# Another order for a two-layer decode kernel: other pairs, other slots, 29 filler matmuls fewer

## The chip, the cores and the metric

The kernel runs on one core of one Trainium2 chip. The metric is the device time of one execution in microseconds (us). TensorE multiplies, VectorE, ScalarE and GpSimd (POOL in the profile) work on vectors, and SyncE (SP) issues the transfers from HBM. Each engine runs its own list of instructions in order and waits on semaphores.

## The reference

Four tokens go through two layers that share their weights. A layer is attention over the last 2048 positions of a key and value cache, and then a gated feed-forward network (FFN). Cut to what matters:

```python
B, D, Hq, Hkv, Dh, W, F = 4, 448, 16, 8, 256, 2048, 1792     # bfloat16
def A(x):                                  # attention, one new position per token
    q = (x @ wq).reshape(B, Hq, Dh)
    k, v = k_cache[:, :, -W:], v_cache[:, :, -W:]            # 8 heads, each for two q heads
    p = softmax(q . k * Dh ** -0.5)
    return (p . v).reshape(B, Hq * Dh) @ wo
def F(x):
    return (silu(x @ w_gate) * (x @ w_up)) @ w_down
for layer in range(2):
    x = x + A(layernorm(x))
    x = x + F(layernorm(x))
```

Both layers read the same caches. For one token and one key-value head the keys are 1 MB and the values 1 MB, so all four tokens and eight heads are 64 MB, more than the on-chip memory holds. A part of what layer 0 has loaded is kept for layer 1, the rest is loaded a second time.

## The kernel before

**Names.** A head's work is written with three digits, token, layer, head: 305 is token 3, layer 0, head 5; 315 is the same head in layer 1. Its keys are K305 and its values the halves V305.0 and V305.1, 512 KB each. Keys come as one load of 1 MB (K305) or as two halves (K305.0, K305.1).

**Groups and steps.** The list PLAN gives the steps; a step has one or more groups, and a group is one head or a pair. In a pair joined by `+` both heads' scores are one run of 32 matmuls; in a pair joined by `&` each member's scores are an instruction block of its own (16 matmuls each), so that the first can start, and give back its keys' slots, before the second's keys are there. For each group:

- VectorE transposes each half of the keys in place (L887, 32 by 32 blocks).
- TensorE makes the scores (L920); VectorE, TensorE and VectorE find and spread the maximum (L936, L941/L944, L950); ScalarE takes the exponential (L954); TensorE turns the probabilities (L969), ScalarE copies them (L978), TensorE and VectorE sum them (L986, L992).
- TensorE multiplies by the values, 8 matmuls for each half (L1001): "the first and second value product".
- ScalarE and VectorE copy the result out (L1017, L1019), TensorE flips it (L1025), VectorE scales it (L1035), and TensorE projects it by the output weights, in columns (L1047) or rows (L1055).

When a token's last head of a layer is projected, its row is added up (L794, L796, L804, L808, L812), normed (L555 to L581; on TensorE L561, "nstat", and L569, "nxe"), and goes through the FFN, as a row (L678 to L706; tokens 1 and 2) or in columns (L740 to L776), and after layer 0 through the next norm and query projection (L615, L621, L631, L638, L647). Token 2 and 3's layer 1 needs that projection's result.

**Slots.** Keys and values live in 31 slots of 512 KB; 7 more are the query weights' place and come free after the last query projection. SLOTS gives, for each load in turn, the slot (a whole key takes two adjacent ones). A load waits until the last reader of the slot's old content is done: the scores for keys, a value product for values. HOLD lists what layer 0 keeps for layer 1 (k keys, v a value half).

**Orders.** SEQ_PE, SEQ_DVE, SEQ_ACT, SEQ_POOL and SEQ_SP list, for each engine, every operation by its number, worked out beforehand and written out. A `w` with a number in SEQ_PE is a filler: one matmul with zero weights and 512 columns into the accumulator A, which adds nothing (L1137, and L543 where a filler follows a filler). The number says between which two uses of A by other engines it has to stand. SyncE issues the loads strictly in order, so a load whose slot isn't free holds up all loads behind it. The wait for a slot is made here:

```python
        for o in order[SP]:
            if o.cells:
                s0 = int(next(slots))
                for s, cell in enumerate(o.cells, s0):
                    cell.append(s)
                    if held[s] is not None:
                        o.deps[last[id(held[s])]] = True
                    elif s >= NPOOL:
                        o.deps.update((d, True) for d in late)
                    held[s] = cell
                self._count(o, f"h{s0}")
```

A whole key is issued at L875, a half at L881, a value half at L897.

Of the kernel before, what the change touches and what calls it, by code (L numbers as in the profile page):

```python
# [43 lines left out]
)  # L44
HOLD = (
# [3 lines left out]
)  # L49
WHOLE = (  # L50
    "000 001 002 003 004 005 006 007 010 011 012 014 100 101 102 103 104 106 107 110 114 116 117 202 203 204 205 "
    "206 207 211 213 215 216 301 302 304 306 307 311 312 313"
# [1149 lines left out]
```

## Time and profile before

| | |
|---|---|
| time, median of 3 runs | 278.19 us (277.27 to 281.54) |
| profiled execution | 280.76 us |
| its span, first to last instruction | 279.0 us |
| mean granted TensorE clock | 0.977 |
| read from HBM | 101.81 MB, 365 GB/s over the span |
| busy: TensorE, VectorE, ScalarE, GpSimd | 244.6, 184.9, 63.5, 80.0 us |
| of TensorE: fillers, 142 and 180 | 54.4 and 53.4 us |
| of VectorE: 86 transpositions of key halves | 104.9 us |

The page gives the whole span in 40 slices: the share that each engine is busy in tenths, the clock that TensorE was granted, and what the transfers moved. A busy TensorE says little, since fillers count as busy. The rows of a stretch give, for each engine, busy us and the number of instructions, then the granted clock, the busy share of the transfer engines and GB/s. The chain of work that ended last gives start, duration and what it was. A group's row gives line, engine, operation, tiles, shape and count, then busy us and the mean ns of one.

### The profile page before, as it was taken

The numbers are of one execution on the slowest core, as the hardware profiler recorded it, in microseconds if no ns is written. First come the engines' busy times: TensorE is split into PE (matmuls) and PEld (weight loads), VectorE is DVE, ScalarE is ACT, GpSimd is POOL, SyncE is SP. The second block draws the span as 40 slices with busy tenths as digits, with TensorE's granted clock in tenths as the row PEclk, the third lists the DMA queues.
The fourth block names the chain that finished last, engine by engine and source line by source line (L and its number), as shares of the span: only waits on it lengthen the run. The fifth ranks groups of instructions, "written<-read, shape, count | busy, mean of one in ns | idle before, by whom it ended". The sixth has DMA issues, their size and how long they took to land.

```text
span 279.0 us, 10606 instructions
## 1 busy us (share of the span) xinstructions
PE 244.6 (88%) x4767; PEld 125.9 (45%) x4587; DVE 184.9 (66%) x574; ACT 63.5 (23%) x173; POOL 80.0 (29%) x223
## 2 busy tenths in 40 slices
PE   3998999889999897999899798898969888998895
PEld 0121232223475454545454344454635547566664
DVE  4666817825702687888948489679678956588941
ACT  0003020101112222332233133123322322232411
POOL 1071021111114222515132432142322334143440
PEclk9999999999999999999999799799998999999998
DMA  7999999999999999999999999999999997899300
GB/s 279 429 416 413 412 398 422 397 400 409 398 392 415 411 411 415 411 406 414 365 414 385 422 414 412 406 325 399 361 375 421 405 391 270 320 403 417 138 2 3
DMA packets 25884, 102.49 MB, mean 367 GB/s; under 512 B 2539, under 2 KB 6639, under 8 KB 21487
## 3 DMA queue, kind: packets, MB, share of 16 engines
q1 hardware_dynamic: 25831, 101.83, 92.4%
q8 instruction: 36, 0.59, 0.9%
q14 instruction: 9, 0.07, 0.1%
q10 hardware_dynamic: 8, 0.00, 0.0%
HBM read 101.81 MB, written 0.00 MB: 365 GB/s over the span
## 4 chain that ended last, share of the span: by engine, by line
PE 23%; DVE 13%; DMA 9%; issue 3%; ACT 2%; POOL 1%; SPq 0%; ACTq 0%
DVE half L887 7%; DMA half<-in_A_v_cache_dram 6%; PE S L920 5%; PE Y L1001 5%; PE A L1137 3%; DMA half<-in_A_k_cache_dram 3%; DVE oh L1019 2%; PE A L543 2%; PE Y L969 1%; PE A L1047 1%; PE Z L740 1%; PE A L1055 1%; ACT wide L621 1%; DVE wide L796 1%; PE Z L615 1%
## 5 line engine op out<-in xcount | busy, mean ns | idle before, releaser
L887 DVE STREAM_TRANSPOSE half<-half 128x1024 uint32<-128x1024 uint32 x86 | 104.9, 1230 | 9.9 <-DMA half<-in_A_k_cache_dram 9.8
L1137 PE MATMUL A<-identb,small 128*128 128x512 bf16 x142 | 54.4, 393 | 3.9 <-DVE A L447 2.9
L1015 POOL TENSOR_TENSOR small<-small 128x2 f32<-128x2 f32 (+1 forms) x48 | 38.4, 803 | 60.9 <-DVE small L992 42.3
L543 PE MATMUL A<-identb,small 128*128 128x512 bf16 x180 | 53.4, 395 | 0.0
L920 PE MATMUL S<-half,qe 128*8 128x128 bf16 (+1 forms) x1536 | 43.8, 243 | 5.7 <-DVE half L887 3.0
L1001 PE MATMUL Y<-half,pT 128*8 128x256 bf16 (+1 forms) x1024 | 43.1, 275 | 4.1 <-DMA half<-in_A_v_cache_dram 1.6
L920 PEld LDWEIGHTS S<-half,qe 128*8 128x8 bf16 x1536 | 29.9, 85 | 20.3 <-DVE half L887 10.7
L954 ACT ACTIVATE praw<-S,small 104x128 bf16<-104x128 f32 (+1 forms) x48 | 19.3, 402 | 79.0 <-DVE small L950 74.9
L1019 DVE SCALAR_TENSOR_TENSOR oh<-oh,small,Y 128x256 bf16<-128x256 bf16 x48 | 22.5, 469 | 15.7 <-ACT oh L1017 15.5
L926 POOL TENSOR_TENSOR qe<-qc,tiny 128x64 bf16<-128x64 bf16 x64 | 18.1, 292 | 47.8 <-PE S L920 35.5
L1017 ACT ACTIVATE oh<-Y 128x256 bf16<-128x256 f32 x48 | 18.4, 382 | 47.0 <-PE Y L1001 36.8
L1001 PEld LDWEIGHTS Y<-half,pT 128*8 128x8 bf16 (+1 forms) x1024 | 19.3, 84 | 17.8 <-issue 5.6
L1137 PEld LDWEIGHTS A<-identb,small 128*128 128x128 bf16 x142 | 14.7, 103 | 17.8 <-issue 10.9
L978 ACT ACTIVATE pT<-Y 128x64 bf16<-128x64 f32 (+1 forms) x48 | 12.4, 257 | 35.0 <-PE Y L969 28.5
L1055 PE MATMUL A<-wo_sb,oT 128*4 128x448 bf16 x188 | 16.5, 360 | 1.8 <-DMA wo_sb<-in_A_wo_dram 1.3
L577 POOL TENSOR_SCALAR st<-st 128x1 f32<-128x1 f32 x16 | 4.2, 265 | 47.6 <-DVE st L567 43.3
L992 DVE TENSOR_REDUCE small<-Y 128x2 f32<-128x32 f32 (+1 forms) x48 | 9.0, 190 | 9.6 <-PE Y L986 8.5
L1082 POOL MEMSET oT<- 128x16 bf16 x38 | 4.1, 111 | 32.3 <-PE A L1055 26.7
L950 DVE TENSOR_REDUCE small<-S 104x1 f32<-104x32 f32 x48 | 8.4, 176 | 6.2 <-PE S L944 6.1
L1035 DVE TENSOR_TENSOR oT<-Y,small 128x4 bf16<-128x4 f32 (+1 forms) x63 | 9.0, 154 | 5.0 <-PE Y L1025 2.1
L936 DVE TENSOR_REDUCE tiny<-S 104x1 bf16<-104x128 f32 (+1 forms) x24 | 7.7, 323 | 5.2 <-PE S L920 5.0
L986 PEld LDWEIGHTS Y<-pT,tiny 128*128 128x128 bf16 x64 | 5.3, 98 | 12.4 <-ACT pT L978 5.9
(139 smaller groups left out, 272.6 us busy)
## 6 DMA issues: line engine op xcount, KB each, us to landing
half<-in_A_v_cache_dram SPq DMA_DIRECT2D x85, 512.0 KB, 11.1
half<-in_A_k_cache_dram SPq DMA_DIRECT2D x31, 1024.0 KB, 11.5
half<-in_A_k_cache_dram SPq DMA_DIRECT2D x24, 512.0 KB, 9.6
wo_sb<-in_A_wo_dram SPq DMA_DIRECT2D x8, 448.0 KB, 17.1
half<-in_A_wq_dram SPq DMA_DIRECT2D x3, 1024.0 KB, 8.7
wd_sb<-in_B_w_down_dram SPq DMA_DIRECT2D x1, 1568.0 KB, 18.4
wg_sb<-in_B_w_gate_dram SPq DMA_DIRECT2D x1, 1344.0 KB, 18.0
wu_sb<-in_B_w_up_dram SPq DMA_DIRECT2D x1, 1344.0 KB, 21.0
```

What stands on the lines that cost most here:

```text
L543: return e.add_instruction(mybir.InstMatmult(start_tensor_calc=start, stop_tensor_calc=stop, ldweights=load, name=nc.get_next_instruction_ ...
L887: return e.transpose(a, a)
L920: last = e.matmul(Sb[s_][qd:qd + 8, 0:32 * 2 * J], lhsT=qe[q_][:, P, ce, :, :].rearrange("p a n -> p (a n)"), rhs=keys(kcs[P], J * x, J, c ...
L926: g.op(POOL, "qe", lambda e, P=P, t=t, kvh=kvh: e.tensor_tensor(qe[q_][:, P, :, :, :], qc[t][:, kvh, :, :].unsqueeze(2).broadcast_to([128, ...
L954: return e.activation(praw[0:R, 0:N].rearrange("p (g r l) -> p g r l", g=J, l=2), Sb[s_][0:R, 0:N].rearrange("p (l g r) -> p g r l", l=2, ...
L978: g.op(SCA, f"pt{n}", lambda e: e.activation(pf, Yb[p_][:, 0:PW], ACT.Copy), r=(f"yp{p_}",), w=(f"pT{pt}",), bank=(f"Y{p_}",))
L1001: last = e.matmul(Yb[p_][32 * gg:32 * gg + M, 256:512], lhsT=pT[pt][:, gg, 2 * a + hv, 4 * P:4 * P + M] if n == 2 else pf[:, 16 * gg + 8 * ...
L1015: g.op(POOL, f"pow{n}", lambda e: e.tensor_tensor(ri[p_][:, 0:2 * n], rs[p_][:, 0:2 * n], expo[:, 1:1 + 2 * n], op=ALU.pow), r=(f"rs{p_}", ...
L1017: g.op(SCA, "oh", lambda e: e.activation(oh[:, :], Yb[p_][:, 256:512], ACT.Copy), r=(f"y{p_}",), w=("oh",), bank=(f"Y{p_}",))
L1019: g.op(DVE, "oho", lambda e: e.scalar_tensor_tensor(out=oh[:, :], in0=oh[:, :], scalar=lomask[:, 0:1], in1=Yb[p_][:, 256:512], op0=ALU.mul ...
L1055: last = e.matmul(Ab[32 * k:32 * k + B, 0:D], lhsT=oT[oi][:, k % 2, k // 2, :], rhs=wo_sb[:, 4 * kvh + k, :], start=False, stop=False, ski ...
L1137: return e.matmul(Ab[:, 0:512], lhsT=w, rhs=rhs, start=False, stop=False, skip_group_check=True)
```

## The change

Only the lists change. In PLAN, two pairs become `&` pairs (117 with 204, 215 with 217) and four become `+` pairs (213 with 216, 214 with 301, 212 with 111, 210 with 310); 203 and 115, and 110 and 305, are now steps of their own. In HOLD, v351 goes and v021 comes: V315.1 is loaded again and V012.1 isn't. In WHOLE, the loads of K110, K206 and K312 become halves, and those of K305, K300, K303, K210, K310 and K315 become whole; the other names that come and go there are of held keys, which aren't loaded. 85 value halves are loaded before and after; whole keys go from 31 to 34, half keys from 24 to 18. The fillers go from 322 to 293. The orders and slots are the same up to the slot of the 38th load; the order of the loads is the same up to the 81st.

```diff
 PLAN = (
     "005+001", "002+000", "006", "007", "003+004", "101 102", "100", "017+015", "016&014", "107 013", "103 105",
-    "106", "104", "010", "202", "201", "200 012", "113&114", "117+204", "203 115", "116", "205", "206 207",
-    "011 302", "110 305", "300", "213&216", "214&301", "303", "215+217", "304", "306+307", "112 211 212&111",
-    "313+317", "314+316", "210&310", "311", "315+312",
+    "106", "104", "010", "202", "201", "200 012", "113&114", "117&204", "203", "115", "116", "205", "206 207",
+    "011 302", "110", "305", "300", "213+216", "214+301", "303", "215&217", "304", "306+307", "112 211 212+111",
+    "313+317", "314+316", "210+310", "311", "315+312",
 )
 HOLD = (
-    "k03 ... v351 v360 v361 v370 v371"
+    "k03 ... v001 v021 v030 ... v360 v361 v370 v371"
 )
 WHOLE = (
-    "... 110 114 116 117 202 203 204 205 206 207 211 213 215 216 301 302 304 306 307 311 312 313"
+    "... 013 014 ... 107 114 117 202 203 204 205 207 210 211 214 217 300 301 302 303 304 305 306 307 310 315 316 317"
 )
 SLOTS = (
-    "0 2 5 13 18 26 7 15 20 28 4 3 10 12 25 23 8 5 17 16 13 14 2 26 7 15 20 26 27 20 4 5 6 21 29 30 26 20 4 6 0 1 "
+    "0 2 5 13 18 26 7 15 20 28 4 3 10 12 25 23 8 5 17 16 13 14 2 26 15 4 20 5 6 26 27 20 22 29 21 6 26 20 0 5 22 "
...
 )
```

SEQ_PE, SEQ_DVE, SEQ_ACT, SEQ_POOL and SEQ_SP are new from the place on where the two programs part, in the second half and a little before. Read back into names, the loads from the 82nd on are, before:

```
V012.1 V012.0 K204 K203 V204.0 V204.1 K205 V205.0 V203.0 V203.1 K206 V205.1 K207 K011 K302 V206.0 V206.1 V207.1
V207.0 K110 V011.0 K305.0 K305.1 V011.1 V302.0 K300.1 K300.0 V302.1 V110.0 V110.1 V305.0 K301 V305.1 V300.1 V300.0
K304 K303.0 V303.0 K303.1 K306 V301.1 V301.0 V303.1 K307 K112.1 K112.0 V306.1 V304.1 V304.0 V307.0 V306.0 V307.1
V211.0 V112.0 K212.0 K111.1 V112.1 K212.1 K111.0 K210.0 V211.1 V212.0 K210.1 V111.0 V212.1 V111.1 K310.0 K315.1
V310.0 K310.1 K315.0 V315.0 K312 V210.0 V210.1 V312.0 V312.1
```

and after:

```
V012.0 K204 V203.1 K203 V203.0 V207.0 K205 K206.1 V204.1 V204.0 V205.0 V205.1 K206.0 V206.0 K207 K011 K302 V206.1
V207.1 K110.1 V011.0 V011.1 K110.0 K305 K300 V302.0 V302.1 V110.0 V110.1 V305.0 K301 V305.1 V303.0 V300.1 K303 V300.0
K304 K306 V301.1 V301.0 V303.1 V306.0 K307 V307.1 V304.0 K112.0 V304.1 V306.1 K112.1 V307.0 K111.0 K212.1 K212.0 V211.0
V112.0 K111.1 V112.1 K210 V212.0 V211.1 V212.1 V111.0 V111.1 K310 K315 K312.0 V210.1 K312.1 V210.0 V310.0 V312.0 V315.0
V312.1 V315.1
```

What frees the slots of the loads that the prediction speaks of (S the scores, P the value products of a group):

| load | before | after |
|---|---|---|
| V200.1 | P of 202 | P of 202, second half |
| K204 | S of 012 | S of 200 and P of 201, first half |
| V203.1 | P of 200 | P of 201, second half |
| K301 | P of 302 and S of 305 | S of 305 |
| K303 | halves: P of 110, P of 300 | S of 300 |
| K304 | S of 300 | P of 305, both halves |
| V304.0 | S of 215+217 | P of 213+216, first half |
| K111.0 | S of 211 | S of 217 |
| K210 | halves: S of 112, S of 212 | P of 112, first half, and S of 112 |
| V211.1 | S of 211 | S of 211 |
| V315.1 | not loaded | P of 211, first half |

On TensorE, after token 3's last layer-0 value products, the order before is: scores of 112, column projections, scores of 211, nstat, first value product of 112, the FFN with nxe in it, second value product of 112. After it is: scores of 112 ahead of the last of token 3's value products, column projections, scores of 211, nstat, nxe, first value product of 112, the FFN's first part, second value product of 112. On VectorE, before, one half of K210 is transposed before and one after the row addition of token 1 (L796) that follows the last query projection; after, both are transposed before it.

More of the change, by code (lines that the diff above doesn't have):

```diff
@@ L40 @@
     "005+001", "002+000", "006", "007", "003+004", "101 102", "100", "017+015", "016&014", "107 013", "103 105",
[3 rows of a table removed]
[3 rows of a table added]
 )
 HOLD = (
[3 rows of a table removed]
[3 rows of a table added]
 )
 WHOLE = (
-    "000 001 002 003 004 005 006 007 010 011 012 014 100 101 102 103 104 106 107 110 114 116 117 202 203 204 205 "
-    "206 207 211 213 215 216 301 302 304 306 307 311 312 313"
+    "000 001 002 003 004 005 006 007 010 011 012 013 014 100 101 102 103 104 106 107 114 117 202 203 204 205 207 "
+    "210 211 214 217 300 301 302 303 304 305 306 307 310 315 316 317"
 )
```

115 rows, old and new, of tables (HOLD, SEQ_ACT, SEQ_DVE, SEQ_PE) are left out of this document.

## The prediction

> **What bounds the kernel now.** I read the page first, then the stream of loads by stretches, then the chain of work that ended last.
>
> ```profile
> span 279.0 us, 10606 instructions
> PE 244.6 (88%) x4767; PEld 125.9 (45%) x4587; DVE 184.9 (66%) x574; ACT 63.5 (23%) x173; POOL 80.0 (29%) x223
> PEclk9999999999999999999999799799998999999998
> DMA  7999999999999999999999999999999997899300
> GB/s 279 429 416 413 412 398 422 397 400 409 398 392 415 411 411 415 411 406 414 365 414 385 422 414 412 406 325 399 361 375 421 405 391 270 320 403 417 138 2 3
> q1 hardware_dynamic: 25831, 101.83, 92.4%
> half<-in_A_v_cache_dram SPq DMA_DIRECT2D x85, 512.0 KB, 11.1
> half<-in_A_k_cache_dram SPq DMA_DIRECT2D x31, 1024.0 KB, 11.5
> half<-in_A_k_cache_dram SPq DMA_DIRECT2D x24, 512.0 KB, 9.6
> ```
>
> The kernel reads 101.83 MB through one queue at about 412 GB/s, so a load of 512 KB (a unit from here on) takes 524288 B / 412 GB/s = 1.27 us. Each slice of the GB/s row is 279.0 / 40 = 6.98 us. The bytes run out in slice 37 (138 of about 412 GB/s, so after a third of it, 258.1 + 2.3 = 260.4 us); the last 18 us are computation. The stream is not full everywhere. Taken by stretches, with an undisturbed one first:
>
> ```profile
> 100.00:120.00 20.00, 17.26 (x412) 9.76 (x404) 16.72 (x44) 5.66 (x19) 6.54 (x17) 1.00 1.02 412
> 132.50:153.50 21.00, 19.00 (x388) 10.04 (x382) 15.51 (x45) 6.27 (x16) 5.11 (x16) 1.00 0.99 389
> 181.00:188.00 7.00, 6.65 (x152) 3.50 (x146) 5.49 (x19) 1.88 (x5) 3.52 (x11) 1.00 0.94 321
> 195.00:209.00 14.00, 11.09 (x253) 6.99 (x248) 9.30 (x27) 4.17 (x10) 4.47 (x14) 0.97 1.00 369
> 230.00:244.00 14.00, 12.92 (x336) 9.33 (x333) 8.28 (x34) 2.88 (x8) 4.19 (x13) 1.00 0.84 293
> ```
>
> The last number is GB/s. Against 412 the four stretches lose 21 × 23/412 = 1.2 us, 7 × 91/412 = 1.5, 14 × 43/412 = 1.5 and 14 × 119/412 = 4.0: 8.2 us in all. A hole appears where a load can't be issued because its slot is freed late, and the chain shows the same from the other side:
>
> ```profile
> 198.48 7.96 DMA half<-in_A_k_cache_dram
> 212.10 9.52 DMA half<-in_A_v_cache_dram
> 230.37 0.59 PE S L920 x29
> 231.83 7.86 DMA half<-in_A_v_cache_dram
> 239.73 0.42 PE Y L1001 x8
> ```
>
> The pieces at 198.48, 212.10 and 231.83 are K303.1, V304.0 and V211.1. The scores of 211 end at 230.96, SyncE then issues K111.0, K210.0 and V211.1, and TensorE goes on with 211 at 239.73. So the second half is bound by a loop: computation frees a slot, SyncE issues, the load lands 8 us later, computation goes on.
>
> **How late a load may be issued.** Two stretches in which the queue had run nearly dry give the time from issue to landing (last column):
>
> ```profile
> half<-in_A_v_cache_dram SPq DMA_DIRECT2D x4, 512.0 KB, 5.5
> half<-in_A_v_cache_dram SPq DMA_DIRECT2D x1, 512.0 KB, 7.3
> ```
>
> They are the four values issued at 181 to 184 us and V303.0, issued at 197.90. So the slot of a load must be free 5.5 to 7.3 us ahead of its turn. With 1.27 us a unit I can read the new order of loads for risk: count the units between the newest load that the freeing instruction, or one before it on its engine, needs, and the landing of the load that reuses the slot. Seven units are 8.9 us and leave 1.6 to 3.4 us for the computation between; four are 5.1 us and leave less than nothing. From V201.0 on, the old order has 19 loads with seven units or fewer, the new one 17.
>
> **The change part by part.**
>
> (a) *The exchanged half.* V002.1 now stays until 012 uses it, so V012.1 is not loaded, and V315.1 is loaded as the very last unit. The bytes are the same. All loads between come one unit, 1.27 us, sooner: **−1.3 us** for everything that waits on them. The price is one slot fewer up to about 144 us. V315.1 at the end is hidden if its landing stays ahead of the products of 315+312, which the chain has at 265.58 (row below), 5 us after the last bytes now. Without that cover it costs up to its 1.27 us. If the sooner stream waits for computation instead, the part gives 0.
>
> (b) *The holes at 181 to 209*, 3.0 us. K303.1 waited for the values of 300, and V304.0 for the scores of 215+217. K303 as a whole load now waits only for the scores of 300, and V304.0 takes a slot of the values of 213+216, a few microseconds sooner. But V110.0, V305.1, V303.0, V300.1 and K304 still stand seven units behind what frees them; K304 is moved behind both values of 305. All 3.0 may go, or these five may lose 1.5 more than now; I take a third of the hole, **−1.0 us**.
>
> (c) *The hole at 230 to 244*, 4.0 us. The old queue stood behind the scores of 112 and of 211. In the new one K210 (1 MB) waits for the first value product of 112, four units behind V112.0 and nine behind V307.0, token 3's last layer-0 value. Its delay from these rows (V306.0 is the value landing at 224.2; 112's two products are the last rows):
>
> ```profile
> 224.20 0.83 PE L1001 MATMUL Y<-half,pT 128*8 128x256 bf16 x24
> 231.54 0.39 PE L1001 MATMUL Y<-half,pT 128*4 128x256 bf16 x8
> 233.02 0.39 PE L1001 MATMUL Y<-half,pT 128*4 128x256 bf16 x8
> ```
>
> Now it ends 231.93 − 224.20 = 7.7 us after token 3's last values begin. The new order has fewer fillers before it but puts the second norm matmul (nxe) ahead of it; working the same steps with their present durations I get 6.7. K210 can then land at 6.7 + 5.5 to 7.3 + 1.27 (its second unit) = 13.5 to 15.3 us; its turn is at 9 × 1.27 = 11.4. The hole is 2.1 to 3.9 us; I take 3.3, **−0.7 us**. Bounds: −4.0 if the product ends within 3 us, and +3 if it ends at 10. Everything behind K210 moves with it.
>
> (d) *The tail.* From 248 us the chain goes through VectorE's transpositions of the last keys:
>
> ```profile
> 248.31 0.61 DVE L796 TENSOR_TENSOR wide<-A,wide 128x448 bf16<-128x448 f32 x1
> 249.35 1.23 DVE L887 STREAM_TRANSPOSE half<-half 128x1024 uint32<-128x1024 uint32 x1
> 260.37 1.23 DVE L887 STREAM_TRANSPOSE half<-half 128x1024 uint32<-128x1024 uint32 x1
> 265.58 1.05 PE Y L1001 x32
> 276.35 0.28 DVE wo_sb L819
> ```
>
> Between 248.31 and 261.60 VectorE does seven transpositions with hardly a gap. In the new order both of K210 stand ahead of the row of 248.31, so six are left: **−1.2 us**, if K210 lands in time for that, else 0. The keys of 312 come two units sooner, which VectorE hides; a hole in (c) grown by 3 us would uncover them. From 265.58 on nothing changes: 13.4 us to the end.
>
> (e) *29 fillers fewer.* 26 of them stood between the first token's FFN row and the next query projection of token 2, 137 to 202 us: 46 before, 20 after.
>
> ```profile
> L1137 PE MATMUL A<-identb,small 128*128 128x512 bf16 x28 | 11.4, 419 | 0.5 <-DVE wide L796 0.5
> L543 PE MATMUL A<-identb,small 128*128 128x512 bf16 x18 | 6.5, 406 | 0.0
> 155.00:158.00 3.00, 1.22 (x13) 0.34 (x11) 0.36 (x2) 0.22 (x1) 1.62 (x2) 0.82 1.00 407
> 158.00:161.00 3.00, 3.00 (x52) 1.32 (x49) 1.87 (x5) 0.97 (x3) 1.05 (x3) 0.62 1.03 426
> 176.00:178.00 2.00, 1.07 (x18) 0.66 (x17) 1.83 (x3) 0.00 (x0) 0.29 (x1) 0.84 1.04 414
> 178.00:181.00 3.00, 3.00 (x38) 1.65 (x35) 1.68 (x5) 0.37 (x1) 0.02 (x1) 0.54 1.04 412
> 206.00:209.00 3.00, 0.66 (x24) 0.61 (x28) 2.54 (x4) 0.68 (x2) 0.00 (x0) 0.85 1.04 418
> ```
>
> Where a filler lies in a wait, taking it away gives nothing, and I take 0. If all 46 − 20 were in the way, 26 × 17.9/46 = 10 us would go; nothing in the chain from 195 to 240 suggests it, it is waits for data. On the other side stands the clock, which the rows price: TensorE was busy 1.22 of 3.00, 1.07 of 2.00 and 0.66 of 3.00 us, and the granted clock fell, to 0.62 and 0.54 in the stretches after. At half clock 3.4 us cost 1.4 to 1.7.
> [...]
>
> (f) *Other pairs.* Two pairs fewer are scored member by member, 215+217 and 117+204 against 213+216, 214+301, 212+111 and 210+310; the matmuls are the same, so 0, hidden under loads either way; a pair that waits for its later member costs a unit, 1.27 us, and one let go early gives as much. Three keys fewer in halves net: the 1 MB loads took 11.5 us to land against 9.6, two queue entries become one, and the first half's transposition can begin 1.27 us later. Token 0's and 2's reordered groups before 172 us, with a hole of 1.2 us: 0, between −1.2 and +2.5.
>
> **The sum.** −1.3 − 1.0 − 0.7 − 1.2 = −4.2 us on the span of 279.0. This execution took 280.76 us, the median of the runs shown is 278.19, 2.6 lower. I take the difference off the median: **274.0 us**.
>
> **The rivals.**
>
> *The clock (slower).* 26 fillers of 0.39 us busy are 10 us of TensorE work out of 65 us that already have three half-speed stretches. That makes three to six more sparse windows, each followed by 3.4 us at half clock for about 1.5 us: +4.5 to +9, so 278.5 to 283, middle 280.5. It decides from the third extra window on, where the gain is eaten. For it: the rows in (e). Against: waits may become shorter too, and a wait for data hides a slow clock. [...]
>
> *Loads issued just in time (slower).* One mechanism: a dry queue behind loads of which the slot is freed late. New places with six units are V200.1, K204 and V203.1 (old: seven or more): up to 2.5 us. K301 and K304, whole, 2.0. K210's hole at 5.5 above mine. Together +10, 284.0 us. It decides from the point where 112's first product ends 8 us or more after V307.0. Against: the values of 201 are now multiplied before token 1's row is added, and free two of these slots sooner.
>
> *A full stream (much faster).* All holes but the first stretch's go: −1.3 − 3.0 − 4.0 − 1.2 = −9.5, 268.7 us. For it: every hole is a late issue. Against: four units between V112.0 and K210.
>
> *Nothing gained*, 278.2: the sooner loads wait for VectorE, busy 16.72 of 20 us at 100 to 120, and the holes only move.
>
> **How the numbers follow.** My forecast 0.42 (271 to 277), clock 0.17, just in time 0.15, full stream 0.18, nothing 0.08. A measurement of this kernel can tell about 2% from no change, here below 272.6 or above 283.8. Faster takes the full stream and 0.13 of my own case: 0.31. Slower takes 0.10 of the just-in-time case and 0.07 of the clock's: 0.17. Within is 0.52. The range for 8 in 10 reaches from just above the full stream to below the just-in-time case, 269.5 to 283.0.
>
> **What would show it.** (a, b) GB/s over 181 to 209 us near 390, and token 3's last layer-0 value product about 2 us sooner than 226. (c) One hole of 2 to 4 us some 8 us after that product, with SyncE waiting for the values of 112 (L1001). (d) Six transpositions between the scores of 314+316 and those of 315+312. (e) At most four stretches of half clock before 212 us. Wrong: more than five such stretches on the chain, new holes at 138 to 150 us, or a wait of TensorE for V315.1 at the end.

## The result and the profile after

The changed kernel is slower by a little: median 281.01 us (278.16 to 286.08, 20 runs) against 279.13 us (276.44 to 282.32, 20 runs) of the kernel before on the same chip. The ratio is 1.0062, 95% interval 1.0033 to 1.0092, so about +1.7 us where I had forecast −4.2. Executions of one kernel spread, the longer ones mostly at a lower clock (kernel before, in the experiments: 0.972 on the mean for the 33 longer ones, 0.987 for the 84 others), so all ratios leave out those of over 1.5% above their kernel's fastest; the one profile below of such a long execution is that of the kernel before with 192 instructions more. The profiled execution took 281.1 us on the device with a span of 279.2; line numbers are one lower than before (L887 is now L886, L1001 is L1000).

The page of the changed kernel, its busy line, granted clock, GB/s and the queue of the instruction packets:

```profile
span 279.2 us, 10561 instructions
...
PE 241.7 (87%) x4738; PEld 126.1 (45%) x4571; DVE 185.4 (66%) x574; ACT 62.1 (22%) x173; POOL 80.2 (29%) x223
...
PEclk9999999999999999999999997999579999896898
...
GB/s 277 424 424 412 413 396 418 398 403 405 401 392 415 410 414 411 414 405 414 394 395 404 416 411 401 369 398 408 400 418 403 407 325 343 271 398 414 55 2 3
...
q8 instruction: 36, 0.59, 0.8%
```

The same five stretches as in the prediction, now of the changed kernel (busy us and count of PE, PEld, DVE, ACT, POOL, then clock, DMA share, GB/s):

```profile
100.00:120.00 20.00, 17.14 (x408) 9.65 (x404) 16.56 (x44) 5.68 (x19) 6.55 (x17) 1.00 1.02 413
132.50:153.50 21.00, 17.63 (x410) 10.54 (x392) 15.10 (x47) 5.69 (x15) 6.06 (x17) 1.00 1.01 397
181.00:188.00 7.00, 5.74 (x130) 3.26 (x123) 6.85 (x13) 2.58 (x7) 1.88 (x7) 1.00 1.03 396
195.00:209.00 14.00, 13.34 (x274) 8.32 (x263) 9.04 (x26) 2.70 (x8) 5.97 (x15) 0.63 1.01 408
230.00:244.00 14.00, 11.20 (x268) 7.25 (x267) 7.17 (x27) 3.61 (x9) 3.29 (x7) 0.88 0.78 304
```

The stream did what I said up to 209 us: 396 and 408 GB/s where it had 321 and 369. But the clock in 195 to 209 is 0.63 where it was 0.97, and the hole at 230 to 244 is hardly smaller (304 against 293 GB/s). Token 3's last layer-0 value product came 3.3 us sooner and the first product of 112 3.8 us sooner than before (231.54); the rows of before, then of after, from the timeline of TensorE:

```profile
225.93 0.40 PE L1001 MATMUL Y<-half,pT 128*8 128x256 bf16 x8
...
261.65 1.07 PE L920 MATMUL S<-half,qe 128*8 128x256 bf16 x32
```

```profile
222.63 0.43 PE L1000 MATMUL Y<-half,pT 128*8 128x256 bf16 x8
227.72 0.39 PE L1000 MATMUL Y<-half,pT 128*4 128x256 bf16 x8
...
261.82 1.06 PE L919 MATMUL S<-half,qe 128*8 128x256 bf16 x32 [0.27 <-DVE half L886]
```

The last row of each kernel is the scores of 315+312: at 261.65 before, at 261.82 now. So 3.8 us of lead at 228 were gone by 262, and the rest of the program is alike. The chain of the changed kernel shows where they went:

```profile
227.72 0.39 PE Y L1000 x8
...
228.60 3.10 PE Z L739 x112
231.71 0.32 PE Y L1000 x8
232.03 0.55 PE Z L775 x17
232.58 2.68 issue
235.26 1.16 PE Z L775 x39
236.45 1.81 PE S L919 x32
...
251.44 0.12 PE S L919 x4
251.56 2.05 issue
253.61 1.67 PE S L919 x28
```

There is no load in it, where the chain of the kernel before had 7.86 us of waiting for V211.1. In its place TensorE stands still twice in the middle of a group of matmuls, behind 17 of the 56 of the FFN's down part and behind 4 of the 32 scores of 210+310, waiting for nothing that the trace names. I call such a pause an idle piece; the chain calls it "issue". A stretch at half clock follows each of the two, the lower two pairs of rows. The upper two pairs are the other stretches at half clock between 80 and 270 us, each with the sparse stretch ahead of it:

```profile
164.28:167.69 3.41, 1.97 (x49) 1.00 (x45) 3.41 (x8) 0.80 (x3) 1.50 (x5) 1.00 1.00 406
167.69:171.10 3.41, 3.18 (x33) 1.27 (x30) 2.43 (x6) 0.50 (x2) 0.72 (x3) 0.50 1.02 411
191.58:194.99 3.41, 2.21 (x55) 1.17 (x47) 2.46 (x8) 2.19 (x4) 1.11 (x3) 1.00 1.03 423
195.00:205.20 10.20, 9.65 (x184) 6.03 (x176) 6.46 (x19) 1.73 (x5) 3.31 (x9) 0.50 1.00 404
232.54:235.95 3.41, 0.73 (x30) 0.69 (x28) 0.91 (x2) 0.00 (x0) 0.00 (x0) 1.00 0.97 383
235.96:239.37 3.41, 3.41 (x64) 2.04 (x61) 1.53 (x12) 0.00 (x0) 0.17 (x1) 0.50 0.20 72
249.60:253.02 3.42, 1.96 (x71) 1.46 (x58) 2.87 (x9) 0.61 (x2) 0.81 (x1) 1.00 1.02 401
253.03:259.85 6.82, 6.22 (x96) 3.72 (x99) 3.33 (x10) 1.62 (x5) 1.49 (x3) 0.50 0.91 367
```

In all, this profile has 23.9 us at half clock between 80 and 270 us, that of before 10.2.

**What the idle pieces are.** The page counts 36 instruction packets of together 0.59 MB, 16 KB each, for 4738 + 4571 = 9309 matmuls and weight loads: 9309/36 = 259 to a packet. Counting the matmul and weight-load records ahead of each piece, the pieces stand at 2733, 4515, 7571 and 8334 here, and at 2733, 4514, 5278, 7575 and 8340 in the kernel before. The differences are whole multiples (3, 7, 9 and 12 times) of 254.3 to 255.2. From these two counts I take 256 instructions a packet, a block from here on, as an estimate. All nine pieces end 1.3 to 1.5 us after the end of an instruction packet: the packet of 232.94 to 233.85 us comes before the end of the first long piece at 235.26, the packet of 251.34 to 252.29 before that of the second at 253.61. So by these records TensorE stands there until its next block of 256 instructions has come. Between 80 and 255 us both kernels fetch 27 such blocks in 175 us, one in 6.5 us; the shortest spacing while loads run is 5.9 us, and where the queue of loads runs dry, at 228 to 240 us, it is 3.5 us here and 4.6 and 5.6 us in the kernel before. So while loads ran, TensorE got no block sooner than 5.9 us after the one before, and at the nine pieces it was through with one before the next had come. The FFN and the scores are the dense places: 112 matmuls with as many weight loads take 3.10 us.

### The profile page after: what moved, and what is told of

Read it like the earlier page. It is cut to its first block, busy times and chain, and to the rows that moved or that the text cites. A ratio compares the mean times of both kernels' runs of the same rounds, so it can differ in the third digit from the quotient of the medians.

```text
span 279.2 us, 10561 instructions
## 1 busy us (share of the span) xinstructions
PE 241.7 (87%) x4738; PEld 126.1 (45%) x4571; DVE 185.4 (66%) x574; ACT 62.1 (22%) x173; POOL 80.2 (29%) x223
## 5 line engine op out<-in xcount | busy, mean ns | idle before, releaser
L886 DVE STREAM_TRANSPOSE half<-half 128x1024 uint32<-128x1024 uint32 x86 | 104.9, 1231 | 7.9 <-DMA half<-in_A_k_cache_dram 7.8
L919 PE MATMUL S<-half,qe 128*8 128x128 bf16 (+1 forms) x1536 | 45.9, 251 | 9.5 <-DVE half L886 3.8
L1136 PE MATMUL A<-identb,small 128*128 128x512 bf16 x126 | 47.7, 388 | 3.3 <-DVE A L446 2.9
L542 PE MATMUL A<-identb,small 128*128 128x512 bf16 x167 | 49.3, 399 | 0.0
L1000 PE MATMUL Y<-half,pT 128*8 128x256 bf16 (+1 forms) x1024 | 45.1, 282 | 2.8 <-DVE small L991 2.1
L919 PEld LDWEIGHTS S<-half,qe 128*8 128x8 bf16 x1536 | 30.0, 87 | 25.4 <-DVE half L886 11.8
L1000 PEld LDWEIGHTS Y<-half,pT 128*8 128x8 bf16 (+1 forms) x1024 | 20.6, 86 | 15.3 <-DVE small L991 5.3
L1054 PE MATMUL A<-wo_sb,oT 128*4 128x448 bf16 x188 | 18.4, 372 | 2.2 <-DMA wo_sb<-in_A_wo_dram 1.4
L1136 PEld LDWEIGHTS A<-identb,small 128*128 128x128 bf16 x126 | 13.1, 104 | 13.8 <-issue 7.8
L1024 PEld LDWEIGHTS Y<-tiny,oh 128*128 128x128 bf16 x96 | 6.8, 101 | 12.2 <-DVE oh L1018 7.1
L935 DVE TENSOR_REDUCE small<-S 104x1 bf16<-104x128 f32 (+1 forms) x24 | 8.0, 334 | 6.1 <-PE S L919 5.9
```

What stands on the lines that cost most here:

```text
L542: return e.add_instruction(mybir.InstMatmult(start_tensor_calc=start, stop_tensor_calc=stop, ldweights=load, name=nc.get_next_instruction_ ...
L886: return e.transpose(a, a)
L919: last = e.matmul(Sb[s_][qd:qd + 8, 0:32 * 2 * J], lhsT=qe[q_][:, P, ce, :, :].rearrange("p a n -> p (a n)"), rhs=keys(kcs[P], J * x, J, c ...
L935: g.op(DVE, "max" + m_, lambda e: e.tensor_reduce(pmax[s_][0:R, :], Sb[s_][0:R, 0:N], AX.X, ALU.max), r=(f"s{s_}",), w=(f"pmax{s_}",), ban ...
L1000: last = e.matmul(Yb[p_][32 * gg:32 * gg + M, 256:512], lhsT=pT[pt][:, gg, 2 * a + hv, 4 * P:4 * P + M] if n == 2 else pf[:, 16 * gg + 8 * ...
L1054: last = e.matmul(Ab[32 * k:32 * k + B, 0:D], lhsT=oT[oi][:, k % 2, k // 2, :], rhs=wo_sb[:, 4 * kvh + k, :], start=False, stop=False, ski ...
```

## The experiments

**1. Moving the block ends by taking early fillers away.** Fillers of stage w1 (up to about 70 us in the trace; the expectations say 60) are left out, always those behind the first of a run, so that each is one instruction (in the profile of before the 142 fillers of L1137 have a weight load each, the 180 of L543 have none).

```diff
- "... 52 w1 w1 w1 w1 w1 w1 w1 w1 w1 w1 w1 w1 w1 w1 w1 56 ..."
+ "... 52 w1 w1 w1 56 ..."    # 60 of the 166 left out; with 120 left out: 52 w1 56
```

> The changed kernel without 60 of the 166 filler matmuls of its first 60 us (w1), where TensorE waits for loads; nothing else differs, so every later TensorE instruction moves 60 places forward in the instruction stream. Theory A (instruction supply): TensorE takes its instructions in blocks of about 256, and the two idle pieces that show no wait (2.68 us at 232.58, 2.05 us at 251.56) stand where a block ended in a dense run of matmuls. The block ends then fall 60 matmuls later in the work: the pieces move to other matmuls and change size, and the time changes by 0.5 to 4 us, most likely down (276 to 280 us). Theory B (clock and missing fillers of the second half): these 60 fillers lie before 60 us, the second half is the same, and the time stays at 281 +/- 0.5. Theory C (the whole key load 210 holds the loads up): same as B, 281 +/- 0.5.

> The changed kernel without 120 of the 166 filler matmuls of its first 60 us: later TensorE instructions move 120 places, about half a block of 256. Theory A: both idle pieces without a wait move by 120 matmuls and weight loads, out of the dense run at 232 us where they stood; the time differs from that with 60 taken away by up to 3 us in either direction, 276 to 282 us. Theories B and C: 281 +/- 0.5, as nothing in the second half differs.

> The control: the kernel before, also without 60 of the early fillers. Theory A: its idle pieces without a wait (1.78 us at 155, 0.92 at 176, 0.72 at 235.6, 0.89 at 253.3) move and change size; the time changes by 0.5 to 3 us in either direction, not by the same amount as in the changed kernel. Theories B and C: no change, 279 +/- 0.5; and if the early fillers themselves cost or save time, the change is the same as in the changed kernel.

> The kernel before without 120 of the early fillers. Theory A: idle pieces without a wait at other places than with 60 taken away, 277 to 282 us, and the difference between the two kernels at equal removal is not the same 1.9 us at 0, 60 and 120. Theories B and C: no change, 279 +/- 0.5, and the difference between the two kernels stays as it is.

Measured: changed kernel −60 284.56 us (ratio to the kernel before 1.0196, 1.0138 to 1.0253) and −120 281.48 (1.0107, 1.0058 to 1.0156); kernel before −60 281.29 (1.0129, 1.0076 to 1.0181) and −120 280.21 (1.0101, 1.0062 to 1.0141). Something early moves a time whose second half is untouched, against B and C. A's guess that the changed kernel would get faster was wrong. And it is no clean shift: the early clock fell too (in the traces of the kernel before, 6.8 us at half clock before 80 us with 60 away and 23.9 with 120, against none; over all its executions the mean clock was 0.966 and 0.944, against 0.986 without the edit on the same chip).

**2 and 4. Moving them with the early columns kept.** The early fillers are cut into pieces: the same columns in more instructions. 122 more is about half a block, 256 a whole one.

```diff
             if g.before == "fw":
+                if g.cut <= 166:
+                    raw_mm(e, Ab[:, 0:256], w, rhs[:, 0:2, :], (128, 128), (0, 0), False, False, False)
+                    return raw_mm(e, Ab[:, 256:512], w, rhs[:, 2:4, :], (128, 128), (0, 0), False, False, False)
                 return raw_mm(e, Ab[:, 0:512], w, rhs, (128, 128), (0, 0), False, False, False)
```

> The kernel before with the same split of 122 early fillers. Theory A: its idle pieces without a wait move too; the time changes by 0.5 us or more, not by the amount of the changed kernel. Theories B and C: no change, ratio 1.000 +/- 0.004, mean clock 0.986 as before.

> The changed kernel; 122 of the 166 fillers of the first 60 us are each issued as two matmuls of 256 columns instead of one of 512. TensorE does the same work at the same places and stays as busy as it was, so its early clock stays high (with fillers taken away it fell to half before 65 us); every later instruction only moves 122 places, about half a block of 256, back in the stream. Theory A (instruction supply, where the blocks end): the idle pieces without a wait at 232 and 251 us move by half a block and the time changes by more than 0.7 us, most likely down to 278 to 280. Theory B (the clock and the fillers missing between 137 and 202 us): no change, ratio to the kernel before 1.006 +/- 0.004, mean clock 0.958 +/- 0.008. Theory C (the whole key load 210): no change.

> The kernel before; 122 early fillers (before 60 us) are each issued as three or four matmuls of 512 columns together, which adds exactly 256 instructions and no work. Theory A1 (what counts is where in the work the blocks of 256 instructions end): a whole block is added, the later blocks end at the same matmuls as in the kernel before, and the time comes back from the +1.0% of half a block to 0.0 +/- 0.4%. Theory A2 (any change to the early part costs about 1%, or the time was a lucky order of the whole): it stays at +1.0 +/- 0.4%. Theory A3 (the rate at which instructions arrive bounds the second half, wherever the blocks end): 0.0 or a little above, as nothing is added behind 60 us, and the half block should have been 0 too.

> The changed kernel with the same 256 early instructions more. A1: the block ends are those of the changed kernel again, ratio 1.006 +/- 0.004, with idle pieces of 2 to 3 us at 232 and 251 us in the same matmuls. A2: 1.010 or more. Theory B (clock): 1.006.

Measured: kernel before 280.88 (1.0103, 1.0063 to 1.0143) at 122 and 278.91 (0.9988, 0.9944 to 1.0033) at 256; changed kernel 280.66 (1.0093, 1.0049 to 1.0137) and 280.26 (1.0061, 1.0021 to 1.0101). For the kernel before A1 holds: half a block costs 1.0%, a whole block nothing, and the two intervals don't touch. The changed kernel can't tell: at 0, 122 and 256 its intervals overlap. TensorE's idle pieces without a named releaser (us in all, times, the longest) show the shift in the kernel before: as it was, then with half a block, then with a whole one.

```profile
PE S L944 <- issue: 1.8, 1, 1.8
PE S L920 <- issue: 0.9, 1, 0.9
PE A L1047 <- issue: 0.9, 1, 0.9
PE Y L1001 <- issue: 0.9, 1, 0.9
PE Z L740 <- issue: 0.7, 1, 0.7
```

```profile
PE S L920 <- issue: 2.9, 4, 1.1
PE Y L1001 <- issue: 2.0, 2, 1.3
PE Z L776 <- issue: 1.8, 1, 1.8
```

```profile
PE S L944 <- issue: 1.5, 1, 1.5
PE S L920 <- issue: 1.4, 2, 1.1
PE Y L1001 <- issue: 1.2, 1, 1.2
PE A L1047 <- issue: 0.9, 1, 0.9
PE Z L740 <- issue: 0.3, 1, 0.3
```

At a whole block they are back at the same five lines. At half a block L944, L1047 and L740 are gone and L776 is new. In the changed kernel with a whole block, A1's "in the same matmuls" came true for only one of the two long pieces: that in the scores of 210+310 is back (1.99 us), that in the FFN's down part is not there:

```profile
233.72 1.57 PE L775 MATMUL Z<-wide,wd_sb 128*128 128x32 bf16 x56
```

TensorE waits 3.1 us for values in that profile instead (0.5 in the changed kernel as it was), and the time is the same 1.006. So that piece of 2.68 us is not by itself what the changed kernel loses.

**3. The fillers.** 26 of before's fillers of 142 to 197 us are left out; and 26 are put into the changed kernel's idle gaps there (18 of stage w10, 4 of w13, 4 of w16, where the expectation below says 22 and 4).

```diff
- "... 740 627 700 w10 w10 629 702 724 742 743 755 756 w10 w10 747 w10 758 w10 w10 w10 w10 w10 w10 749 w10 ..."
+ "... 740 627 700 w10 w10 629 702 724 742 743 755 756 747 758 749 w10 ..."          # before, 38 -> 12
- "... 629 739 754 741 ..."
+ "... 629 739 w10 w10 754 741 ..."                                                   # after, 12 -> 38, in gaps
```

> The kernel before with 26 of its 38 fillers of stages w10, w13, w15 and w16 (142 to 197 us) taken away, as many as the changed kernel has there; order, pairs and loads are those of before. Theory B: the mean clock falls from 0.986 to about 0.96 and the time rises by 2 to 4 us, to 281 to 283. Theory A: the clock between 140 and 200 us hardly matters; the time changes by up to 1.5 us in either direction, through the moved block ends alone. Theory C: no change, 279 +/- 0.5. What I forecast for taking the fillers away was 0.

> The changed kernel with 26 fillers put back into TensorE's idle gaps of 0.3 to 0.9 us between 143 and 195 us (22 of stage w10, 4 of w13, four of these 26 of w16), so that the number of fillers there is that of before. Theory B: the granted clock rises from 0.958 to 0.975 or more and the time falls by 2 to 4 us, to 277 to 279. Theory A: the later block ends move by some 40 instructions, the clock matters only behind the idle pieces; the time changes by up to 2 us in either direction, and the idle pieces of over 1.5 us after 225 us stay or move by 40 places. Theory C: no change.

Measured: kernel before without them 281.71 (1.0118, 1.0056 to 1.0181), mean granted clock over its executions 0.963 (0.983 with them); changed kernel with them 283.70 (1.0192, 1.0133 to 1.0251), clock 0.958 (0.958 without). B forecast the first rightly, clock included, and failed the second: putting fillers back raised no clock and cost 1.3% more. Each of the two also moves later block ends by some 40 places, so what of the first is clock and what is place stays open. What the second shows is that 26 fillers in these gaps bring back neither the clock nor the time; fillers at the places that they have in the kernel before were not tried.

**4b. More instructions behind 140 us.** Each late filler is issued as four matmuls of 128 columns.

```diff
+            if g.cut > 244:
+                ... # one of 128 columns as the filler was (with its weight load or without), then:
+                for c in (1, 2, 3):
+                    ins = raw_mm(e, Ab[:, 128 * c:128 * c + 128], w, rhs[:, c:c + 1, :], (128, 128), (0, 0), False, False, False)
+                return ins
```

> The kernel before with its 78 fillers behind 140 us each issued as four matmuls of 128 columns instead of one of 512: 234 instructions more, hardly any work. A3 (rate of arrival: 256 instructions per 6.2 us or so while loads run): up to 234/256 x 6.2 = 5.7 us more, if all of the added ones fall where TensorE lives from hand to mouth; at least half of it, +2.8 us (ratio 1.010 to 1.020). A1 (only where the blocks end): like any shift, -0.3 to +1.2%, no more. Theory B (clock): as many columns in the fillers, so no change.

> The changed kernel with its 49 fillers behind 140 us issued as four matmuls each: 147 instructions more. A3: up to 147/256 x 6.2 = 3.6 us on top of 1.006, ratio 1.012 to 1.019, and less than what the kernel before gains by its 234. A1: 1.003 to 1.018, like any shift. Theory B: 1.006.

Measured: kernel before 284.74 (1.0188, 1.0134 to 1.0243), changed kernel 281.82 (1.0101, 1.0051 to 1.015). For the kernel before the time is what the rate of arrival (A3) forecast, and its whole interval lies above A1's 1.2%. The mean clock fell as well, from 0.980 to 0.965, so how much of the cost is arrival and how much clock is not shown. Its idle pieces without a releaser are 11.2 us in all against 5.2; the three largest groups:

```profile
PE S L920 <- issue: 3.4, 3, 1.6
PE A L1055 <- issue: 2.3, 1, 2.3
PE Z L776 <- issue: 2.1, 1, 2.1
...
```

For the changed kernel the interval fits A1 and A3 alike.

**5. A quarter and three quarters of a block.** As in 2, with 64 and 192 instructions more.

```diff
+                    for c, n in (((0, 1), (1, 1), (2, 2)) if g.cut2 <= N3 else ((0, 2), (2, 2)) if g.cut2 <= N2 else ((0, 4),)):
+                        ins = raw_mm(e, Ab[:, 128 * c:128 * (c + n)], w, rhs[:, c:c + n, :], (128, 128), (0, 0), False, False, False)
```

> The kernel before with 64 early instructions more (64 fillers before 60 us as two matmuls of half the columns). Theory A1 (where the blocks end): a quarter of a block; between 0 and half a block nothing fixes it but that the kernel stood near its best place at 0: +0.3 to +1.5%. Without A1: 0.0 +/- 0.4%. For the lost gain: D1 (the gain is there, the old place was lucky): over shifts of 0, 64, 122 and 192 the changed kernel is faster by 0.5% or more on the mean. D2 (the gain went elsewhere): the two means are within 0.4%.

> The changed kernel with 64 early instructions more. D1: ratio to the kernel before of 0.990 to 1.002 here or at 192, as its blocks then end elsewhere than in the dense runs at 232 and 251 us. D2: 1.004 to 1.015, like 0 (1.006) and 122 (1.009).

> The kernel before with 192 early instructions more (three quarters of a block). A1: 0.0 to +1.2%, and back to 0 at 256.

> The changed kernel with 192 early instructions more. D1: 0.990 to 1.002 here or at 64. D2: 1.004 to 1.015.

Ratios to the kernel before, with those of 2 and 4, the mean granted clock over the timed executions, two landings from each profile's records of the loads, and the idle pieces without a releaser that start behind 222 us in each profile:

| early instructions added | 0 | 64 | 122 | 192 | 256 |
|---|---|---|---|---|---|
| before: ratio | 1 | 1.0067 | 1.0103 | 1.0031 | 0.9988 |
| after: ratio | 1.0062 | 1.0007 | 1.0093 | 1.0148 | 1.0061 |
| before: clock | 0.983 | 0.973 | 0.978 | 0.977 | 0.984 |
| after: clock | 0.958 | 0.961 | 0.963 | 0.952 | 0.959 |
| before: token 3's last layer-0 value / last load of all, us | 225.4 / 262.3 | 224.4 / 262.0 | 222.4 / 260.1 | 222.3 / 260.3 | 224.6 / 261.2 |
| after: the same | 221.2 / 261.1 | 221.3 / 259.1 | 222.1 / 262.9 | 221.6 / 262.3 | 222.8 / 260.8 |
| before: idle pieces behind 222 us, us | 1.6 | 2.3 | 3.1 | 3.3 | 1.5 |
| after: the same | 4.7 | 4.7 | 3.5 | 4.8 | 2.0 |

The intervals of 64 and 192 are ±0.5%. Experiment 1 fits these rows only in part: 120 taken away is 136 added but for a block, and gave 1.0101 and 1.0107, like 122; 60 away is 196 added, and gave 1.0196 in the changed kernel, also its worst, but 1.0129 in the kernel before, where 192 gave 1.0031. The early clock, which fell in experiment 1, may be why.

Over the four places 0, 64, 122 and 192 the means are 1.0050 for before and 1.0078 for after, a difference of +0.3 ± 0.3%. On the means D2 is right, though at 64 alone the changed kernel came out where D1 had it. The place of the block ends moves either kernel by up to 1.0 and 1.4%, and the gain of 1.5% that I forecast isn't there at the mean either. At 64 the changed kernel equals the kernel before (0.9957 to 1.0058); no version beat it. How the place acts is shown less well. In the kernel before the idle pieces are shortest at 0 and 256, where it is fastest. In the changed kernel they don't go with the time: 4.7 us at 64, its fastest place, and 2.0 us at 256.

**6. Taking TensorE work out of the stretch.** Of the first layer's FFNs of token 0 (77 to 85 us) and of token 3 (229 to 239 us), 128 of 168 matmuls are left out in each. With their weight loads that is a block of 256 instructions at each of the two places, where the expectations count only the second; so the later blocks end at the same matmuls.

```diff
-                for cc in range(c0, c1):
-                    for fc in range(NFC):
+                for cc in (range(c0, c1) if end else (c0,)):
+                    for fc in range(1 if cc == 3 and not end else NFC):
...
-                    for fc in range(NFC):
+                    for fc in range(NFC if end else 2 if cc else 4):
```

> The kernel before with 128 of the 168 matmuls of the first layer's FFN of tokens 0 and 3 (at 231 to 239 us) left out, 256 instructions with their weight loads; loads, order and all other work stay. Theory L (the loop of loads sets the end, as I forecast): the FFN lies beside the wait for V211.1 on the chain (7.86 us from 231.83), so 0 to -1.0 us, ratio 0.996 to 1.002. Theory T (TensorE sets the end from 222 us on, load holes or not): what was taken is 128 x 28 ns = 3.6 us of TensorE, and the ratio falls to 0.984 to 0.991.

> The changed kernel with the same 128 matmuls left out. In its trace the FFN itself stands on the chain, from 228.60 to 236.42, with an idle piece of 2.68 us in it. Theory T: -3.6 us of matmuls and up to -2.7 us of the idle piece, ratio 0.984 to 0.995. Theory L: 0 to -1.0 us, ratio 1.002 to 1.007. Mixed (L in the kernel before, T in the changed one: the change filled the hole with loads but put TensorE's work in its place): before 0.996 to 1.002 and this one 0.984 to 0.995.

Measured: kernel before 280.07 (1.0058, 1.0018 to 1.0098), changed kernel 280.21 (1.0065, 1.0026 to 1.0104). T's fall shows in neither: 3.6 us of TensorE work less in the stretch bought nothing, and that the kernel before came out 0.6% slower, none forecast. T is not refuted by it, since the clock fell with the work: both traces have 6.8 us at half clock from about 233 us on, where the kernel before had none and the changed kernel 3.4, and the mean clock fell from 0.983 to 0.965 and from 0.958 to 0.947. The timeline of the changed kernel without that work, at the scores of 210+310 and of 315+312:

```profile
249.90 0.29 PE L919 MATMUL S<-half,qe 128*8 128x256 bf16 x4
253.20 1.59 PE L919 MATMUL S<-half,qe 128*8 128x256 bf16 x28 [3.01 <-issue]
...
260.92 1.13 PE L919 MATMUL S<-half,qe 128*8 128x256 bf16 x32 [0.32 <-DVE half L886]
```

It reaches the block's end at 250.19 instead of 251.56, 1.4 us sooner, and goes on at 253.20 instead of 253.61: 1.0 of the 1.4 us went into a longer idle piece (3.01 against 2.05). That is one way in which a lead is lost here. The scores of 315+312 began 0.9 us sooner than in the profile without the edit.

## Why the prediction was wrong

**(a) and (b), the sooner stream: right in mechanism, wrong in worth.** I had token 3's last layer-0 product 2 us sooner and it was 3.3 (over the five profiles of the table, its last value landed 2.0 us sooner on the mean, 223.8 and 221.8). The last load of all landed at 261.2 and 261.3 us on the mean, since V315.1 now stands behind the rest. But the lead reached the last keys: those of 312 had landed at 253.4 instead of 256.2 us on the mean, and in the profile of the changed kernel 8.4 us ahead of their scores, against 4.3 before. In all ten profiles the program ends 17.3 to 17.5 us after the scores of 315+312 begin, and these began at 260.7 to 265.4 us before and at 261.1 to 263.5 after. So the failed step is "All loads between come one unit, 1.27 us, sooner: −1.3 us for everything that waits on them": the loads came sooner, and the end did not wait for them. I booked a time of arrival in the middle as time at the end.

**(c), the hole: its place was right, its size and worth were not.** The first product of 112 ended at 228.11, 6.9 us after V307.0's landing (worked out at 6.7), and K210 was issued then. K210 and V212.0 lost 1.8 us together, less than the 3.3 that I took. But V111.0, which waits for the scores of 212+111, came 2.7 us late, behind the idle piece at 232.58, and the sum has no term for that wait; K310 lost 0.9 more. Up to K310 that is 5.4 us lost, against 4.2 up to K310.0 before, where I had booked −0.7. And the row that I quoted for the hole showed TensorE busy 12.92 of 14 us. From 222 to 262 it was busy 36.06 of 40 us before at full clock, and 34.03 after at 0.87:

```profile
222.00:262.00 40.00, 36.06 (x888) 24.20 (x874) 28.27 (x92) 11.00 (x30) 15.15 (x41) 1.00 0.91 350
```

```profile
222.00:262.00 40.00, 34.03 (x813) 22.29 (x809) 26.41 (x84) 9.89 (x27) 11.81 (x32) 0.87 0.85 329
```

A hole in the stream under an engine that is busy nine tenths has little idle time to give back, though fillers count in it (20 of them, about 6.6 us, before). "Bound by a loop" of computation and loads was a reading of the chain alone.

**(d), the tail: six transpositions as said, no gain.** The scores of 315+312 began at 261.82 instead of 261.65. For 4.8 us VectorE now makes no transposition between them. For 2.85 of these it waits for the scores of 210+310 (L919), which ended late, at 255.28, behind the second idle piece; three of the six in the timeline of VectorE:

```profile
249.24 2.36 DVE L886 STREAM_TRANSPOSE half<-half 128x1024 uint32<-128x1024 uint32 x2
...
255.33 0.43 DVE L935 TENSOR_REDUCE small<-S 104x1 bf16<-104x256 f32 x1 [2.85 <-PE S L919]
...
256.42 1.24 DVE L886 STREAM_TRANSPOSE half<-half 128x1024 uint32<-128x1024 uint32 x1
```

**(e), the fillers at 0.** This is the other step that failed: "taking it away gives nothing, and I take 0". In the kernel before, leaving 26 fillers out cost 1.2%, 3.3 us, and the clock fell from 0.983 to 0.963. That having them would help the changed kernel is not borne out. What the term also left out is the instruction: a filler with a weight load (142 of the 322, L1137) is two instructions of a block's estimated 256, and by the count its removal moves every later block end. (f) was never tried by itself.

**The rival with the clock** had the right side and nearly the right time, 280.5 us. Four more stretches of 3.4 us at half clock in the profile (23.9 against 10.2 us) are inside its three to six. The three that it reckons from, in the profile of before, with the stretch ahead of each:

```profile
153.48:156.89 3.41, 1.69 (x75) 1.30 (x64) 1.04 (x4) 0.22 (x1) 2.34 (x4) 1.00 1.01 414
156.89:160.30 3.41, 3.35 (x39) 1.10 (x40) 1.87 (x5) 0.75 (x2) 0.70 (x1) 0.50 1.04 428
173.96:177.37 3.41, 2.21 (x71) 1.42 (x71) 2.78 (x7) 0.97 (x3) 1.30 (x4) 1.00 1.03 410
177.37:180.78 3.41, 3.41 (x42) 1.76 (x36) 1.93 (x6) 0.37 (x1) 0.00 (x0) 0.50 1.02 407
204.68:208.09 3.41, 1.05 (x29) 0.60 (x29) 1.63 (x3) 0.28 (x1) 0.99 (x5) 1.00 1.01 412
208.09:211.50 3.41, 3.16 (x76) 2.15 (x76) 2.76 (x5) 0.91 (x3) 0.00 (x0) 0.50 1.02 419
```

That each further sparse stretch brings 3.4 us at half clock was my estimate from these three pairs (TensorE busy 1.69, 2.21 and 1.05 of 3.41 us, then 3.41 us at 0.50); so was the 1.5 us for each, and no run shows that price. At every place of the table the changed kernel's mean clock is lower, by 0.011 to 0.026. The cause that the rival names, the missing fillers, stays open. For it: 13.7 of the 23.9 us lie at 167 to 206 us, behind sparse places (busy 1.97 and 2.21 of 3.41 us) of the stretch that lost 26 fillers, and hold no idle piece; and the same loss lowered the clock of the kernel before. Against it: the other two sparse places, those before 235.96 and 253.03 (busy 0.73 and 1.96), hold the idle pieces at block ends, and putting 26 fillers back raised no clock.

How much the clock could be is seen in the timed executions. Of those of the kernel before, without any edit, that the ratios of the experiments rest on (several chips), the 32 with a mean clock of 0.99 or more took 277.3 us on the mean, the 37 from 0.98 up 278.5 and the 15 from 0.97 up 280.0. The four of the changed kernel from 0.97 up took 280.0 too. So at one clock the two kernels are alike, and a difference as large as the whole +1.7 us goes with the clock. That is no proof of cause: half clock followed both long idle pieces above (2.68 and 2.05 us), so the pieces and the clock come together here, and the changed kernel's other nine executions, at lower clocks, took no longer (280.1). How much of the +1.7 us is the clock and how much the idle pieces was not separated.

Of the signs that I had named, the stretches at half clock before 212 us stayed within four (one of 3.4 us and one of 10.2); two more came behind 230 us, where I had not looked. Holes at 138 to 150 us and a wait for V315.1 did not show.

**What I would now say:** the change brings the loads 2 to 3 us ahead, down to the last keys, and the end does not wait for them: it comes 17.3 to 17.5 us after the scores of 315+312, which wait for TensorE's and VectorE's own work, and in these runs that work was not sooner. The old order had its block ends at one of its best places, 0.5% below its mean over the four. A change of 45 matmuls and weight loads moves the later ends off it. The new order at a quarter of a block more is level with it (1.0007), but its interval reaches to 1.0058, so it is not clear of the 1.0062 without the shift. That the place of the block ends matters is shown, by half a block against a whole one in the kernel before and by 64 against 192 in the changed kernel. What takes the rest of the forecast 1.5%, TensorE's idle pieces, the clock, or the order of work on VectorE, is argued from the chain and from the clocks, and not shown.

## What to carry to other kernels

Before a lead in a stream of loads is booked as time, read how busy each engine is from there to the end, and look for the next thing that would be late; a lead that isn't followed to the last instruction is worth nothing yet. Compare the granted clocks of many executions too, and not only their times. When a tuned order of many small matmuls is compared with another, add a quarter, a half and a whole block of 256 instructions in an early idle stretch of both: a difference under 1% may be only the place where the blocks end, as here half a block cost the kernel before 1.0%. Idle time in the middle of a group of matmuls, with no releaser, repeated at multiples of about 255 records of matmuls and weight loads (254.3 to 255.2 in the two profiles), was the sign here.

## What the hardware showed that I had not expected

- From 80 to 255 us of the two profiles, no two instruction packets began closer than 5.9 us to each other while loads filled the queue; where it ran dry, at 228 to 240 us, they began 3.5 us apart after and 4.6 and 5.6 us before. At nine ends of blocks TensorE stood still, up to 2.68 us, and went on 1.3 to 1.5 us after the packet's end; in experiment 6 it stood 3.01 us at one.
- A shift by half a block (122 instructions) cost the kernel before 1.0%, by a whole block (256) −0.1% (0.9944 to 1.0033).
- 234 instructions more behind 140 us, with the same columns, cost 1.9%, 5.2 us, with the clock down by 0.015. At 6.5 us a block their arrival alone would be an estimated 234/256 × 6.5 = 5.9 us.
- In the profile after, twice a stretch of 3.4 us in which TensorE stood at a block's end (busy 0.73 and 1.96 us) was followed by half clock, for 3.41 and 6.82 us.
